# The first fifty microseconds of a fused attention and expert kernel: the order of its opening work

## The chip, the cores and the metric

The kernel runs on one core of a Trainium2 chip. The core has five engines that each run their own instruction list in order: the tensor engine (PE, matmuls and transposes), the vector engine (DVE), the scalar engine (ACT), GpSimd (POOL) and the sync engine (SP), which here only issues transfers. They wait for one another through semaphores. The metric is the device time of one execution in microseconds (us); lower is better. The kernel before takes 721.48 us (median of 3 runs, 721.1 to 725.26).

## The reference: what is computed

A block-sparse attention feeds a mixture of experts. Attention has 4 batches, 8 heads, 768 positions and a head width of 64; its mask keeps, for each block of 32 queries, the neighbouring key blocks, the first and the last block, and three sampled ones. Each of the 3072 resulting rows of 512 goes to the one expert of eight with the highest gate logit.

```python
scores = scale * np.matmul(q, k.transpose(0, 1, 3, 2))
mask = np.abs(blk_i - blk_j) <= window
mask = mask | (blk_i == 0) | (blk_j == 0) | (blk_i == n_blocks - 1) | (blk_j == n_blocks - 1)
for qb in range(n_blocks):
    for kb in sampled_blocks[qb]:
        mask[qb * block:(qb + 1) * block, kb * block:(kb + 1) * block] = True
scores = np.where(mask, scores, -1000000000.0)
attn = np.exp(scores - np.max(scores, axis=-1, keepdims=True))
attn = attn / (np.sum(attn, axis=-1, keepdims=True) + 1e-09)
x = np.matmul(attn, v)            # then (B, H, S, D) -> (B*S, H*D)
...
logits = x @ w_gate
expert_idx = np.argmax(logits, axis=1)
# per expert e, on its rows:  y = np.maximum(x @ w1[e], 0.0) @ w2[e]
return gate_w[:, None] * y
```

## The kernel before

Heads are worked on in 16 pairs, `pairs[n]`, and each pair in two halves of 384 queries: a step is (n, half). A step computes scores for six chunks of 128 keys (`scores`), takes their exponential, adds them up (`esum`), multiplies with v (`attend`), and a step later divides by the sums (`divide`). The mask is applied in one of two ways. Either a second pair of small matmuls adds a penalty to the scores (`oh` says which block a key belongs to, `pen` which blocks a query may not see), or, for the "late" chunks 0 to 2, POOL multiplies the exponential with a table of zeros and ones (`mask`), which `make_late` computes once. `ps_s` is a rotation of three buffers in PSUM, which the tensor engine writes.

```python
lend(lent, ps_s=3)
...
def load(b, pr):
    for src, nm in ((k, "k_sb"), (q, "q_sb")):
        t = ld.tile([P, NCH, 2, D], F32, name=nm)
        for hh in range(2):
            queue = nc.scalar if nm == "q_sb" and (b, pr) == (0, 0) else nc.sync
            queue.dma_start(t[:, :, hh, :], src[b, 2 * pr + hh].rearrange("(p c) d -> p c d", p=P))
    ...                                          # v on nc.sync

def make_mask(pool):
    ...                                          # samp_i fetched on nc.scalar
    load(0, 0)
    ...
    nc.vector.memset(oh[:], 1.0)
    for ... in (six bounds):
        nc.gpsimd.affine_select(out=allow[:], in_=allow[:], ...)
    nc.gpsimd.iota(kb_i[:], ...)
    for half in range(2):
        part = oh[half * D : (half + 1) * D]
        for base, cm, st, sp in ((0, -BLK, 1, NCH), (BLK - 1, BLK, -1, -NCH)):
            nc.gpsimd.affine_select(out=part, in_=part, ...)
    nc.vector.tensor_copy(kb[:], kb_i[:])
    nc.vector.tensor_copy(samp[:], samp_i[:, :, 0])
    for r in range(NR):
        nc.vector.scalar_tensor_tensor(allow[:], in0=kb[:], scalar=samp[:, r : r + 1], in1=allow[:], ...)
    nc.vector.tensor_copy(allow2[:, :NB], allow[:])
    nc.vector.tensor_copy(allow2[:, D : D + NB], allow[:])
    for c in range(30):                          # keeps the tensor engine at work
        nc.tensor.transpose(idle[:, 0, :P], ident[:], ident[:])
    for half in range(2):
        nc.tensor.matmul(bm[:, half, :CW], lhsT=allow2[:], rhs=oh[:NB, half * HC : (half + 1) * HC, :], ...)
    for half in range(2):
        nc.vector.tensor_scalar(pen[:, half * CW : (half + 1) * CW], bm[:, half, :CW], ...)

def make_mix():
    nc.scalar.dma_start(wg[:], moe_w_gate.rearrange("(c p) e -> p c e", p=P))
    nc.gpsimd.memset(mix[:], 0.0)
    for pr in range(NPR):
        nc.gpsimd.tensor_copy(mix[:, pr, :P], ident[:])
        nc.gpsimd.tensor_copy(mix[:, pr, P:], wg[:, pr, :])

def make_late():
    for j, c in enumerate(LATE):                 # LATE = (0, 1, 2)
        bm = upper["ps_s"].tile([P, 2, 512], F32, name="bm", tag="s")
        for half in range(2):
            nc.tensor.matmul(bm[:, half, :CW], lhsT=oh[:D, c, :], rhs=pen[:D, cols], ...)
        nc.vector.tensor_single_scalar(mask[:, j, :]..., bm[:, :, :CW], 0.0, op=ALU.is_ge)

def turn(b, pr, which):                          # 12 transposes of k or q into tp (a ps_s buffer), then
    for j in range(2):
        to, got = dst.rearrange("p (c j t) -> p j c t", j=2, t=D)[:, j], tp[:, j, :CW]...
        if (b, pr, which) == (0, 0, 1):
            nc.vector.tensor_copy(to, got)
        else:
            nc.scalar.copy(to, got)

def scores(n, half, c):
    late = c in LATE and 0 < n < NA              # NA = 12
    ...                                          # two matmuls per chunk, k with q (L252)
    for hh in range(0 if late else 2):           # the penalty (L255)
        nc.tensor.matmul(s[:, hh, :CW], lhsT=oh[r, c, :], rhs=pen[r, cols], ...)
    nc.scalar.activation(e, s[:, :, :CW], AF.Exp, scale=scale)            # L257
    if late:
        nc.gpsimd.tensor_tensor(e, e, m..., op=ALU.mult)                  # L261
    if c >= 3:
        ...                                      # sums on nc.vector (L267)

for which in range(2):
    turn(0, 0, which)
for i, (n, half) in enumerate(steps):
    ...                                          # loads two pairs ahead
    if 0 < i and n + 1 < len(pairs):
        turn(*pairs[n + 1], half)
    for c in range(NCH):
        scores(n, half, c)
    if i == 0:
        make_mix()
        route_consts()                           # small constants on POOL; `t` also uses nc.vector (L459, L460)
    if i > 0:
        divide(*steps[i - 1])                    # sums over keys by matmul (L290), reciprocal
    for c in ORDER:
        attend(n, half, c)
    if i == 0:
        make_late()
        turn(*pairs[1], 0)
    ...                                          # rows out, gates, then the experts
```

The lists of PE, DVE and POOL follow the order of the program text; that of ACT does so from the loop on.

Of the kernel before, what the change touches and what calls it, by code (L numbers as in the profile page):

```python
# [12 lines left out]
ALU = mybir.AluOpType  # L13
# [4 lines left out]
def kernel(  # L18
# [11 lines left out]
    nc = tc.nc  # L30
    P = 128
    B, H, S, D = q.shape
    BLK = 32
# [71 lines left out]
    def load(b, pr):  # L105
        got = []
        for src, nm in ((k, "k_sb"), (q, "q_sb")):
            t = ld.tile([P, NCH, 2, D], F32, name=nm)
            for hh in range(2):

                queue = nc.scalar if nm == "q_sb" and (b, pr) == (0, 0) else nc.sync
                queue.dma_start(t[:, :, hh, :], src[b, 2 * pr + hh].rearrange("(p c) d -> p c d", p=P))
            got.append(t)
        t = ld.tile([P, 2, NCH, D], F32, name="v_sb", bufs=3)
        nc.sync.dma_start(
            t.rearrange("p h c d -> p h (c d)"), v[b, 2 * pr : 2 * pr + 2].rearrange("h (p c) d -> p h (c d)", p=P),
        )
        got.append(t)
        loaded[(b, pr)] = got
# [17 lines left out]
    def make_mask(pool):  # L137

        halves = bass.DRamTensorHandle(sampled_blocks.tensor.name, (2 * NB * NR,), I32)
        samp_i = pool.tile([NB, NR, 2], I32, name="samp_i")  # L140
        nc.scalar.dma_start(
            samp_i.rearrange("a b c -> a (b c)"), bass.AP(tensor=halves, offset=0, ap=[[2 * NR, NB], [1, 2 * NR]]),
        )
        load(0, 0)

        warm = pool.tile([P, 1], F32, name="warm")
        nc.scalar.activation(warm[:], ones[:, :1], AF.Exp)

        allow = pool.tile([NB, NB], F32, name="allow")
        nc.vector.memset(allow[:], 1.0)  # L150
        nc.vector.memset(oh[:], 1.0)
        allow2 = pool.tile([NB, P], BF16, name="allow2")
        nc.vector.memset(allow2[:], 0.0)
        for base, cm, step, fill in (
            (1, -1, 1, 0.0), (1, 1, -1, 0.0), (-1, 1, 0, 1.0), (NB - 2, -1, 0, 1.0), (-1, 0, 1, 1.0), (NB - 2, 0, -1, 1.0),
        ):
            nc.gpsimd.affine_select(
                out=allow[:], in_=allow[:], compare_op=ALU.is_ge, fill=fill, base=base, channel_multiplier=cm,
                pattern=[[step, NB]],
            )  # L160
        kb_i = pool.tile([NB, NB], I32, name="kb_i")
        nc.gpsimd.iota(kb_i[:], pattern=[[1, NB]], base=0, channel_multiplier=0)
        for half in range(2):
            part = oh[half * D : (half + 1) * D]
            for base, cm, st, sp in ((0, -BLK, 1, NCH), (BLK - 1, BLK, -1, -NCH)):
                nc.gpsimd.affine_select(
                    out=part, in_=part, compare_op=ALU.is_ge, fill=0.0, base=base, channel_multiplier=cm,
                    pattern=[[st, NCH], [sp, P]],
                )
        kb = pool.tile([NB, NB], F32, name="kb")  # L170
        nc.vector.tensor_copy(kb[:], kb_i[:])
        samp = pool.tile([NB, NR], F32, name="samp")
        nc.vector.tensor_copy(samp[:], samp_i[:, :, 0])
        for r in range(NR):
            nc.vector.scalar_tensor_tensor(
                allow[:], in0=kb[:], scalar=samp[:, r : r + 1], in1=allow[:], op0=ALU.is_equal, op1=ALU.max,
            )
        nc.vector.tensor_copy(allow2[:, :NB], allow[:])
        nc.vector.tensor_copy(allow2[:, D : D + NB], allow[:])

        idle = upper["ps_s"].tile([P, 2, 512], F32, name="idle", tag="s")
        for c in range(30):
            nc.tensor.transpose(idle[:, 0, :P], ident[:], ident[:])
        bm = upper["ps_s"].tile([P, 2, 512], F32, name="bm", tag="s")
        for half in range(2):
            nc.tensor.matmul(
                bm[:, half, :CW], lhsT=allow2[:], rhs=oh[:NB, half * HC : (half + 1) * HC, :], start=True, stop=True,
            )
        for half in range(2):
            nc.vector.tensor_scalar(  # L190
                pen[:, half * CW : (half + 1) * CW], bm[:, half, :CW], scalar1=-MASKED, scalar2=MASKED, op0=ALU.mult, op1=ALU.add,
            )

    def make_mix():
        nc.scalar.dma_start(wg[:], moe_w_gate.rearrange("(c p) e -> p c e", p=P))
        nc.gpsimd.memset(mix[:], 0.0)
        for pr in range(NPR):
            nc.gpsimd.tensor_copy(mix[:, pr, :P], ident[:])
            nc.gpsimd.tensor_copy(mix[:, pr, P:], wg[:, pr, :])
# [21 lines left out]
    def turn(b, pr, which):  # L221

        src = loaded[(b, pr)][which]
        dst = work.tile([P, S], F32, name="qT" if which else "kT")
        turned.setdefault((b, pr), {})[which] = dst
        tp = upper["ps_s"].tile([P, 2, 512], F32, name="tp", tag="s")

        for c in range(NCH):
            for j in range(2):
                r = slice(j * D, (j + 1) * D)  # L230
                nc.tensor.transpose(tp[:, j, c * D : (c + 1) * D], src[r, c].rearrange("p h d -> p (h d)"), ident[r, r])  # L231
        for j in range(2):
            to, got = dst.rearrange("p (c j t) -> p j c t", j=2, t=D)[:, j], tp[:, j, :CW].rearrange("p (c t) -> p c t", t=D)

            if (b, pr, which) == (0, 0, 1):
                nc.vector.tensor_copy(to, got)  # L236
            else:
                nc.scalar.copy(to, got)

    rt = {}  # L240
    es, ops_, esums, xbs, s_alls = {}, {}, {}, {}, {}
# [1 line left out]
    def scores(n, half, c):  # L243

        b, pr = pairs[n]
        kT, qT = turned[(b, pr)][0], turned[(b, pr)][1]
        cols = slice(half * CW, (half + 1) * CW)
        late = c in LATE and 0 < n < NA
        s = upper["ps_s"].tile([P, 2, 512], F32, name="s")
        for hh in range(2):  # L250
            r = slice(hh * D, (hh + 1) * D)
            nc.tensor.matmul(s[:, hh, :CW], lhsT=kT[r, c * P : (c + 1) * P], rhs=qT[r, cols], start=True, stop=late)  # L252
        for hh in range(0 if late else 2):
            r = slice(hh * D, (hh + 1) * D)
            nc.tensor.matmul(s[:, hh, :CW], lhsT=oh[r, c, :], rhs=pen[r, cols], start=False, stop=True)  # L255
        e = e_slot(n, half, c)
        nc.scalar.activation(e, s[:, :, :CW], AF.Exp, scale=scale)  # L257
        es[(n, half, c)] = e
        if late:
            m = mask[:, LATE.index(c), cols]  # L260
            nc.gpsimd.tensor_tensor(e, e, m[:, None, :].to_broadcast([P, 2, CW]), op=ALU.mult)  # L261
        if c >= 3:
            if c == 3:
                esums[(n, half)] = work.tile([P, 2, CW], F32, name="esum")
            t = esums[(n, half)]
            for c_ in {3: (0,), 4: (4, 1), 5: (5, 2)}[c]:
                nc.vector.tensor_add(t[:], es[(n, half, 3)] if c == 3 else t[:], es[(n, half, c_)])  # L267
# [719 lines left out]
    for i, (n, half) in enumerate(steps):  # L987
        if half == 1 and n + 2 < len(pairs):
            load(*pairs[n + 2])
        if 0 < i and n + 1 < len(pairs):  # L990
            turn(*pairs[n + 1], half)
        for c in range(NCH):
            scores(n, half, c)
        if i == 0:
            make_mix()
            route_consts()
        if i > 0:
            divide(*steps[i - 1])
        for c in ORDER:
            attend(n, half, c)  # L1000
        if i == 0:
            make_late()
            turn(*pairs[1], 0)
        if "gates" in rt:
            gate_weights(*rt.pop("gates"))
        if n > 0:
            rows_out(n - 1, half)

        if (n, half) == (NA, 1):
            ranks("A", 0, TA)  # L1010
        if (n, half) == (NA + 1, 0):
            count("A")
            layout_a()
            for i_ in range(2):
                fetch(i_, 1)
                fetch(i_, 2)
        if (n, half) == (NA + 1, 1):
            slots_a()
        if n == NA + 2:
            one_hots("A", rt["slA"], TA, KA, half)  # L1020
        if (n, half) == (NA + 3, 0):
            tokens("A", TA, KA)
            for i_ in range(3):
                gather(i_)
        if n + 1 == len(pairs) and half == 1:
            turn_x(0)
# [171 lines left out]
```

## Time and profile before

| what | before |
|---|---|
| device time, median of 3 | 721.48 us (721.1 to 725.26) |
| profiled span | 720.0 us |
| PE busy | 695.5 us, 97% |
| DVE busy | 437.0 us, 61% |
| ACT busy | 271.7 us, 38% |
| POOL busy | 189.7 us, 26% |
| mean granted PE clock | 0.987 |

The profile is of one execution. A row of its order-of-time view gives the start, the time from the first to the last of so many like instructions, the engine, the line of the kernel, the operation, output and inputs, their shapes, the count, and in brackets how long the engine had been idle and what it had waited for. An engine name with q is its instruction queue, which issues transfers. A row of waits gives who waited for whom, the total, the number of times and the longest. A row of the stretches view gives the window, its length, the busy time of PE, its weight loads, DVE, ACT and POOL with instruction counts, the granted PE clock, and the share and rate of the DMA engines.

The chain of work that ended last, by engine:

```profile
PE 55%; issue 33%; POOL 5%; DVE 3%; DMA 1%; ACT 1%; POOLq 0%; ACTq 0%; another core or an unknown queue 0%; DVEq 0%
```

### The profile page before, as it was taken

The page shows a single profiled execution, that of the slowest core. Times are in us where ns is not written, and L with a number is a line of the kernel's source. Part 1 is how long each engine was busy: PE and PEld are TensorE (multiplying, and loading weights), DVE is VectorE, ACT ScalarE, POOL GpSimd, SP SyncE. Part 2 cuts the span into 40 slices and gives each one's busy share as a digit, 9 for nine tenths or more (in the row PEclk, how much of TensorE's full clock was granted, in tenths as well). Part 3 has the DMA queues.
Part 4 walks back from the last instruction along what each step waited for, and adds up shares of the span by engine and source line. Part 5 has one row for each costly group of instructions (what it writes and reads, how often), then busy time and mean ns, then how long its engine had stood idle before and what let it go on. Part 6 is the DMA issues. An engine that isn't in the chain of part 4 may idle for free.

```text
span 720.0 us, 12889 instructions
## 1 busy us (share of the span) xinstructions
PE 695.5 (97%) x5008; PEld 454.1 (63%) x5008; DVE 437.0 (61%) x828; ACT 271.7 (38%) x456; POOL 189.7 (26%) x180
## 2 busy tenths in 40 slices
PE   8699999999999999999999999999999999999993
PEld 5355555555555555555677776778687967777861
DVE  5399999999999998999748025820228012902200
ACT  3365675567566755765411110111111111111110
POOL 3344554565456540000202112101130013011210
PEclk9799999999999999999999999999999999999997
DMA  8122332233323322194378999996999499979950
GB/s 198 45 66 70 89 88 63 48 92 88 87 70 90 88 65 47 47 361 152 83 253 297 307 327 355 355 338 222 374 396 382 137 364 399 397 254 383 396 192 18
DMA packets 114569, 145.52 MB, mean 202 GB/s; under 512 B 56228, under 2 KB 72676, under 8 KB 114469
## 3 DMA queue, kind: packets, MB, share of 16 engines
q1 hardware_dynamic: 107968, 129.84, 54.6%
q0 software_dynamic: 4368, 14.02, 5.2%
q8 instruction: 53, 0.87, 0.5%
q10 hardware_dynamic: 2132, 0.41, 0.3%
q14 instruction: 48, 0.39, 0.2%
HBM read 131.47 MB, written 12.94 MB: 201 GB/s over the span
## 4 chain that ended last, share of the span: by engine, by line
PE 55%; issue 33%; POOL 5%; DVE 3%; DMA 1%; ACT 1%; POOLq 0%; ACTq 0%; another core or an unknown queue 0%; DVEq 0%
PE s L252 17%; PE op L277 17%; PE hp L833 6%; PE sp L290 4%; PE xr L310 3%; PE zp L847 3%; PE s L255 3%; PE tp L231 2%; POOL out_dram L862 2%; POOL xg L765 1%; DMA q_sb<-in_q_dram 1%; ACT ea L257 1%; DMA wg<-in_moe_w_gate_dram 1%; DVE orB L695 0%; POOL ea L885 0%
## 5 line engine op out<-in xcount | busy, mean ns | idle before, releaser
L261 POOL TENSOR_TENSOR ea<-ea,mask 128x768 f32<-128x768 f32 x66 | 120.4, 1851 | 116.9 <-ACT ea L257 101.5
L257 ACT ACTIVATE ea<-s 128x768 f32<-128x768 f32 x192 | 146.1, 815 | 9.4 <-PE s L255 6.1
L252 PE MATMUL s<-qT,kT 64*128 64x384 f32 x768 | 148.0, 492 | 1.3 <-DVE qT L236 1.2
L833 PEld LDWEIGHTS hp<-xgT,w 128*128 128x128 f32 x1216 | 138.5, 192 | 9.5 <-issue 6.4
L833 PE MATMUL hp<-xgT,w 128*128 128x128 f32 x1216 | 141.4, 276 | 2.6 <-ACT hT L840 1.6
L814 DVE STREAM_TRANSPOSE xgT<-xg 32x128 f32<-32x128 f32 x208 | 62.9, 302 | 128.5 <-DMA xg<-x_rows,gB 87.3
L267 DVE TENSOR_TENSOR esum<-esum,ea 128x768 f32<-128x768 f32 x128 | 125.4, 980 | 12.0
L277 PE MATMUL op<-ea,v_sb 128*64 128x384 f32 x768 | 129.3, 486 | 0.0
L847 PE MATMUL zp<-w,hT 128*128 128x512 f32 x256 | 112.7, 594 | 0.0
L277 PEld LDWEIGHTS op<-ea,v_sb 128*64 128x64 f32 x768 | 55.1, 137 | 68.8 <-issue 65.6
L252 PEld LDWEIGHTS s<-qT,kT 64*128 64x128 f32 x768 | 68.3, 189 | 41.6 <-ACT ea L257 17.0
L297 DVE RECIPROCAL r<-ss 128x128 f32<-128x128 f32 x96 | 82.2, 912 | 0.0
L847 PEld LDWEIGHTS zp<-w,hT 128*128 128x128 f32 x256 | 47.5, 190 | 54.6 <-issue 54.4
L840 ACT ACTIVATE hT<-hp 128x512 f32<-128x512 f32 x36 | 21.5, 598 | 116.9 <-PE hp L833 96.7
L862 POOL DMA_INDIRECT out_dram<-zo,sB x14 | 14.1, 1006 | 166.0 <-ACT zo L852 119.0
L282 ACT COPY oT<-op 128x384 f32<-128x384 f32 x32 | 15.4, 480 | 104.2 <-PE op L277 104.2
L852 ACT ACTIVATE zo<-zp,xg 128x512 f32<-128x512 f32 x16 | 11.0, 689 | 100.7 <-PE zp L847 100.7
L267 DVE TENSOR_TENSOR esum<-ea 128x768 f32<-128x768 f32 x32 | 35.7, 1117 | 14.8 <-ACT ea L257 14.7
L255 PE MATMUL s<-pen,oh 64*128 64x384 bf16 x252 | 41.6, 326 | 0.0
L940 DVE STREAM_TRANSPOSE ea<-ea 32x128 f32<-32x128 f32 x84 | 21.7, 285 | 28.8 <-DMA ea<-x_rows,gB 28.1
L298 DVE TENSOR_TENSOR oT<-oT,r 128x384 f32<-128x384 f32 x32 | 30.2, 943 | 1.1
L310 PEld LDWEIGHTS xr<-mix,oT 128*64 128x64 f32 (+1 forms) x372 | 24.0, 139 | 10.7 <-issue 10.6
(282 smaller groups left out, 546.3 us busy)
## 6 DMA issues: line engine op xcount, KB each, us to landing
w<-in_moe_w_dram SPq DMA_DIRECT2D x50, 2048.0 KB
k_sb<-in_k_dram SPq DMA_DIRECT2D x32, 192.0 KB
v_sb<-in_v_dram SPq DMA_DIRECT2D x16, 384.0 KB
x_rows<-xb SPq DMA_DIRECT2D x16, 384.0 KB
q_sb<-in_q_dram SPq DMA_DIRECT2D x30, 192.0 KB
sums<-ss SPq DMA_DIRECT2D x32, 3.0 KB
q_sb<-in_q_dram ACTq DMA_DIRECT2D x2, 192.0 KB
xg<-x_rows,gB POOLq DMA_INDIRECT x15
```

Source lines behind the costliest of these rows:

```text
L252: nc.tensor.matmul(s[:, hh, :CW], lhsT=kT[r, c * P : (c + 1) * P], rhs=qT[r, cols], start=True, stop=late)
L255: nc.tensor.matmul(s[:, hh, :CW], lhsT=oh[r, c, :], rhs=pen[r, cols], start=False, stop=True)
L257: nc.scalar.activation(e, s[:, :, :CW], AF.Exp, scale=scale)
L261: nc.gpsimd.tensor_tensor(e, e, m[:, None, :].to_broadcast([P, 2, CW]), op=ALU.mult)
L267: nc.vector.tensor_add(t[:], es[(n, half, 3)] if c == 3 else t[:], es[(n, half, c_)])
L277: nc.tensor.matmul(op[hh * D : (hh + 1) * D, :], lhsT=v_sb[:, hh, c, :], rhs=e[:, hh, :], start=(c == ORDER[0]), stop=(c == ORDER[-1]),)
L297: nc.vector.reciprocal(r[:, m * P : (m + 1) * P], ss[:, m * P : (m + 1) * P])
L298: nc.vector.tensor_mul(oT[:], oT[:], r[:])
L310: nc.tensor.matmul(xr[j * M_ : (j + 1) * M_, m, :], lhsT=oT[:, m * P + j * M_ : m * P + (j + 1) * M_], rhs=mix[:, pr, :], start=True, stop ...
L814: nc.vector.transpose(xT[d, :, t], xg[t, :DM].rearrange("p (c q) -> p c q", c=DB)[:, :, d])
L833: nc.tensor.matmul(hp[:, m, :], lhsT=st[i]["w1"][:, c, fb * P : (fb + 1) * P], rhs=st[i]["xT"][:, c, :], start=(c == 0), stop=(c == DB - 1),)
L847: nc.tensor.matmul(zp[:], lhsT=st[i]["hT"][:, fb, :], rhs=st[i]["w2"][:, fb, :], start=(fb == 0), stop=(fb == FB - 1),)
```

## The change

It rearranges the opening; what is computed stays the same.

- The tables of the late masks are made after the third chunk of the very first scores, not after the first attention. With them at hand, the second step (0, 1) also uses the late form: no penalty matmuls for its chunks 0 to 2, but three multiplications on POOL.
- The gate weights `wg` are fetched on the sync queue right after the first pair's loads, so that POOL need not wait for them in `make_mix`.
- The table `oh` is made for 64 partitions and copied to the other 64 by ACT, which leaves POOL two selects fewer.
- The first q loads move from the scalar queue to the sync queue, behind k and ahead of v.
- The first pair's transposes are copied out by halves of the columns rather than by interleaved parts, so that the first scores need one copy of k and one of q.
- The warming transposes are 22, not 30.

```diff
@@ load
-                queue = nc.scalar if nm == "q_sb" and (b, pr) == (0, 0) else nc.sync
-                queue.dma_start(t[:, :, hh, :], src[b, 2 * pr + hh].rearrange("(p c) d -> p c d", p=P))
+                nc.sync.dma_start(t[:, :, hh, :], src[b, 2 * pr + hh].rearrange("(p c) d -> p c d", p=P))
@@ make_mask
         load(0, 0)
+        nc.sync.dma_start(wg[:], moe_w_gate.rearrange("(c p) e -> p c e", p=P))
...
-        nc.vector.memset(oh[:], 1.0)
+        nc.vector.memset(oh[:D], 1.0)
...
-        for half in range(2):
-            part = oh[half * D : (half + 1) * D]
-            for base, cm, st, sp in ((0, -BLK, 1, NCH), (BLK - 1, BLK, -1, -NCH)):
-                nc.gpsimd.affine_select(
-                    out=part, in_=part, compare_op=ALU.is_ge, fill=0.0, base=base, channel_multiplier=cm,
-                    pattern=[[st, NCH], [sp, P]],
-                )
+        for base, cm, st, sp in ((0, -BLK, 1, NCH), (BLK - 1, BLK, -1, -NCH)):
+            nc.gpsimd.affine_select(
+                out=oh[:D], in_=oh[:D], compare_op=ALU.is_ge, fill=0.0, base=base, channel_multiplier=cm,
+                pattern=[[st, NCH], [sp, P]],
+            )
+        nc.scalar.copy(oh[D:], oh[:D])
...
-        for c in range(30):
+        for c in range(22):
@@ make_mix
-        nc.scalar.dma_start(wg[:], moe_w_gate.rearrange("(c p) e -> p c e", p=P))
@@ turn
+        to, got = dst.rearrange("p (c j t) -> p j c t", j=2, t=D), tp[:, :, :CW].rearrange("p j (c t) -> p j c t", t=D)
         for j in range(2):
-            to, got = dst.rearrange("p (c j t) -> p j c t", j=2, t=D)[:, j], tp[:, j, :CW].rearrange("p (c t) -> p c t", t=D)
-            if (b, pr, which) == (0, 0, 1):
-                nc.vector.tensor_copy(to, got)
+            if (b, pr) == (0, 0):
+                cs = slice(j * HC, (j + 1) * HC)
+                (nc.vector.tensor_copy if which else nc.scalar.copy)(to[:, :, cs], got[:, :, cs])
             else:
-                nc.scalar.copy(to, got)
+                nc.scalar.copy(to[:, j], got[:, j])
@@ scores
-        late = c in LATE and 0 < n < NA
+        late = c in LATE and (n, half) != (0, 0) and n < NA
@@ the loop
         for c in range(NCH):
             scores(n, half, c)
+            if (i, c) == (0, 2):
+                make_late()
...
         if i == 0:
-            make_late()
             turn(*pairs[1], 0)
```

## The prediction

> **What bounds the kernel now.** I first read the page's slices of the span and its list of what the tensor engine (PE) waited for over the whole run.
>
> ```profile
> PE   8699999999999999999999999999999999999993
> ...
> PEclk9799999999999999999999999999999999999997
> ```
>
> ```profile
> PE tp L231 <- DVE mask L207: 6.0, 1, 6.0
> PE hp L833 <- ACT hT L840: 1.6, 4, 0.5
> PE idle L183 <- POOL ident L73: 1.4, 1, 1.4
> PE s L252 <- DVE qT L236: 1.2, 1, 1.2
> ```
>
> PE is busy in every slice except the first two and the last, and the granted clock falls in the second slice. The largest wait of the run by far is one 6.0 us wait on the masks of line 207. From 45 us to 500 us PE is never idle for a noticeable time, so time saved ahead of that passes through to the end, and nothing else in this change can. So I read the order-of-time view of the first 50 us.
>
> ```profile
> 15.44 0.42 ACTq L195 DMA_DIRECT2D wg<-in_moe_w_gate_dram  x1
> ...
> 19.13 0.66 POOL L199 COPY mix<-wg 128x8 f32<-128x8 f32 x1 [11.57 <-DMA wg<-in_moe_w_gate_dram]
> ...
> 19.35 1.15 PE L206 MATMUL bm<-pen,oh 64*128 64x384 bf16 x6
> ...
> 25.28 0.18 DVE L459 TENSOR_SCALAR t<-t 128x24 int32<-128x24 int32 x1 [5.55 <-POOL t L456]
> ...
> 25.45 2.68 DVE L207 TENSOR_SCALAR mask<-bm 128x768 bf16<-128x768 f32 x3
> ...
> 26.46 0.91 PE L231 MATMUL tp<-ident,k_sb 64*128 64x64 f32 x12 [5.96 <-DVE mask L207]
> ```
>
> Read from the bottom. PE cannot transpose the second pair's k at 20.5 because all three `ps_s` buffers hold `bm`. Those are freed by the vector engine's (DVE) mask operations, which stand in its program behind `t` (L459). `t` needs the GpSimd (POOL) iota of L456, the last but few of 6 us of POOL constants, and these stand behind the copies of `wg`, whose transfer was issued only at 15.44 and awaited at 19.13. The late transfer, carried through two in-order engines, becomes PE's gap. The stretches view shows the after-effect:
>
> ```profile
> 20.50:26.50 6.00, 0.04 (x2) 0.04 (x2) 1.22 (x4) 0.00 (x0) 4.93 (x33) 0.63 0.00 1
> 26.50:35.30 8.80, 8.71 (x60) 4.97 (x60) 2.24 (x3) 5.61 (x9) 0.29 (x3) 0.67 0.39 89
> ```
>
> The column after POOL is the clock. One-us windows show 0.50 from 22 us until about 32.2 us: PE works at half rate for 5.7 us after it has resumed (26.46 to 32.2), which loses about 2.9 us more.
>
> Lastly the opening, where PE waits for `allow` and then for q:
>
> ```profile
> 2.95 3.65 POOL L166 TENSOR_SCALAR_AFFINE_SELECT oh<-oh 64x768 bf16<-64x768 bf16 x4
> ...
> 3.94 2.68 DVE L175 SCALAR_TENSOR_TENSOR allow<-kb,samp,allow 24x24 f32<-24x24 f32 x3
> ...
> 7.31 0.49 PE L186 MATMUL bm<-oh,allow 24*128 24x384 bf16 x2 [0.67 <-DVE allow L179]
> ...
> 8.49 0.59 PE L231 MATMUL tp<-ident,q_sb 64*128 64x64 f32 x12 [0.17 <-DMA q_sb<-in_q_dram]
> ...
> 9.11 1.02 DVE L236 COPY qT<-tp 128x384 f32<-128x384 f32 x2 [0.25 <-PE tp L231]
> ...
> 10.28 0.92 PE L252 MATMUL s<-qT,kT 64*128 64x384 f32 x4 [1.21 <-DVE qT L236]
> ```
>
> A DVE operation on 24x24 elements takes 0.89 us here: each ends with the POOL select beside it (POOL starts at 2.95, 3.88, 4.80, 5.73; DVE at 3.94, 4.80, 5.73). By the chain of waits q landed at 8.35.
>
> **What the Trainium skill says.** "SBUF — State Buffer", section "Who interferes with whom": DVE and GpSimd share one port pair as an exclusive lock, taken by a DVE copy or scalar operation in a two-port mode or by one with two SBUF inputs against a GpSimd operation that reads. The 0.89 us per tiny operation agrees. "VectorE: DVE Perf Modes", section "Why PSUM operands drop a tier": a PSUM source rules the two-port mode out. The mask operations agree: three of 0.949 to 0.951 us, while POOL worked beside the first and not the last. So moving them beside POOL's constants should not slow them. "DMA: Bandwidth & Descriptors", section "Queues, rings and completion order": each DMA engine goes round robin between the queues that have work. The trace agrees: in 3.5 to 4.0 us the scalar queue moved 506 packets and the sync queue 26, and in 6.5 to 7.0 it was 82 to 197, with v already in the sync queue. "TensorE: Matmul & The Clock Gate", section "What's actually happening": an idle window drops PE to half clock and sustained work restores it; the 0.50 from 22 us to 32.2 us agrees.
>
> **The change part by part.**
>
> (a) *Half the table's selects.* Two selects (2 x 0.91 us) leave POOL, which ends `oh` at 4.74. The following 0.55 us memset and 0.29 us copy of `mix` move up. DVE's second and third step on `allow` then lock against those instead: ends about 5.4 and 5.7, the two casts about 6.0. `bm` starts about 6.05 instead of 7.31. The new scalar-engine (ACT) copy of 64x768 runs about 4.8 to 5.6, when ACT is idle (4.01 us before 8.36). The 22 warming transposes end near 5.5 (the thirty end at 6.64; the last six took 0.82 us, so eight fewer take off 1.1 us): not in the way.
>
> (b) *q on the sync queue ahead of v.* 3072 packets of 256 B must land for k and q. With both queues the trace counts some 2540 of these by 5.5 us; the rest at some 900 per us ends near 6.1. The last q packets ran until about 7.75 and q was released at 8.35, so 0.6 us of tail: landed near 6.7 if q no longer shares with v. Then k transposes start at 6.5, q's at 7.15, and end at 7.75.
>
> (c) *Column halves.* The first scores need only the first of the two 0.5 us qT copies: 7.8 + 0.5 + 0.15 = 8.5 instead of 10.28. Gain of (a) to (c): 1.8 us, my least certain term (0.8 to 2.2).
>
> (d) *Masks amid the scores.* The exponentials are 0.81 us each and begin 1.1 us after the first score: 9.6, 10.4, 11.2, 12.0. The three `bm` pairs (0.32 each) follow the third score at 10.95 and wait for exponential ends: last one at about 12.4. Mask operations (0.95) at 11.5, 12.4, 13.4; scores 3, 4, 5 each need one of their buffers: 12.5, 13.4, 14.4 to 15.2. Scores to attention took 5.04 us before (10.28 to 15.32) and takes about 6.8 now: 8.5 + 6.8 = 15.3. So the move costs 1.75 us here, 1.15 of it paid at 19.35 before. Attention 4.03 us: 19.35, the same moment as before.
>
> (e) *No wait.* The second pair is transposed at once, at full clock: 2 x 0.52 us (the chain's figure at 40.04) to 20.5. Before: 19.35 + 1.15 + 5.96, then 1.86 to 28.32.
>
> (f) *Masked second block.* Scores of (0,1) are now 3 x 0.65 + 3 x 0.81 = 4.4 us, having shed 6 x 0.16 us; the buffers wait for ACT (kT and qT copies 0.86 each, then the exponentials), about 0.2 us more: the sums' matmul (L290) starts at about 25.1 instead of 35.30.
>
> POOL takes 3 x 1.87 us for this. With `wg` queued behind v it should land near 8 to 9; copies and constants (1.7 + 4.4 us up to the iota) end near 15; `t` follows DVE's last sum near 19.5; the last 1.2 us of constants end before 21. The first masked block's exponential ends near 22.5, POOL multiplies until 28.2, and attention wants the third at 29.2. It fits with 1 us to spare.
>
> Sum: 35.30 - 25.1 = 10.2 us. From there everything is as before, including the weight fetches, which PE's progress releases. 721.48 - 10.2 = 711.3; I allow 0.2 for frayed edges: **711.5 us**, 1.4% less.
>
> **The rivals.** *The head start does not come*: q lands near 8.3 regardless, since DMA engines are busy from 2.7 us on either way. For it: the stretch at 155 GB/s near 4.5 us, which I cannot explain. Against: v's packets ran before q was done. It leaves 0.5 us of 1.8: 712.8. *GpSimd becomes the bound*: `wg` in 32-byte runs took 3.6 us from issue alone; behind loads it might land at 13 us or later, pushing the constants past 22.5 and the multiplies into attention. POOL has 7 us of slack there, so it would take more than that: 712 to 714. *The masks stall the scores or the warm clock is lost* (eight fewer warming transposes): about 3.4 us of half rate would cost 1.7: 713.2. *DVE takes over*: it was 95% busy from 100 to 200 us, and PE's gap had let it catch up. By my times its sums of (0,1) end near 29.8, when PE leaves attention, as before (39.7 against 39.97): no loss expected, but 1 to 2 us if they pile up.
>
> **Range and chances.** The 5.96 us wait and 2.9 us of half clock are firm; the shed 1.0 us nearly so. Uncertain are the head start (-1.0, +0.4), stalls (1), POOL (1) and the runs' own spread (721.1 to 725.26). I take 709.3 to 714.8. A gain over 2% needs below 707.05, or 4 us beyond my sum: 3%. Slower by 2%: 1%. Within 2%: 96%.
>
> **What would show it.** In the changed profile: no PE wait on line 207's mask beyond 0.5 us, a clock of 1.00 from 20 to 35 us; the first scores at 8.5 and the L290 sums at 25.1; mask operations at 11 to 14; q landed below 7; POOL's first multiply by 23. Wrong would be a new PE wait on POOL near 27 us, or a gain at 25 us that is gone at 260.

## The result, and the profile after

The changed kernel takes 712.02 us (median of 4 runs, 711.38 to 712.32) against 722.34 us for the kernel before in the same comparison: a ratio of 0.985 with a 95% interval of 0.9818 to 0.9883. The prediction was 711.5, in a range of 709.3 to 714.8. The profiled span fell from 720.0 to 710.6 us.

The slices of the span of the changed kernel, tensor engine (PE) and granted clock:

```profile
PE   8999999999999999999999999999998999999993
...
PEclk9999999999999999999999999999999999999997
```

The dip in the second slice is gone from both rows. What PE waited for over the whole run, longest first:

```profile
PE hpu L949 <- DMA w<-in_moe_w_dram: 3.5, 2, 1.9
PE idle L181 <- POOL ident L73: 1.4, 1, 1.4
PE hp L831 <- ACT hT L838: 1.4, 3, 0.5
PE s L250 <- DVE qT L234: 0.7, 1, 0.7
```

The 6.0 us wait on the masks has vanished. In first place stands a wait for expert weights that the profile of before did not show; more of it below. In order of time, the lines that answer to the chain shown of before:

```profile
4.42 0.47 SPq L143 DMA_DIRECT2D wg<-in_moe_w_gate_dram  x1
...
8.97 0.19 POOL L196 COPY mix<-wg 128x8 f32<-128x8 f32 x1 [3.40 <-DMA wg<-in_moe_w_gate_dram]
...
11.84 2.69 DVE L204 TENSOR_SCALAR mask<-bm 128x768 bf16<-128x768 f32 x3 [2.70 <-PE bm L203]
...
19.61 0.59 PE L228 MATMUL tp<-ident,k_sb 64*128 64x64 f32 x12
...
22.67 5.57 POOL L259 TENSOR_TENSOR ea<-ea,mask 128x768 f32<-128x768 f32 x3 [1.31 <-ACT ea L255]
...
25.26 0.87 PE L288 MATMUL sp<-esum,ones 128*64 128x384 f32 x4
```

The weights are there at 8.97 instead of 19.13, the mask operations run at 11.84, PE transposes the second pair at 19.61 without a wait, and the sums' matmul, the mark that the prediction counted by, starts at 25.26 (25.1 predicted) instead of 35.30. The opening:

```profile
3.93 1.35 DVE L173 SCALAR_TENSOR_TENSOR allow<-kb,samp,allow 24x24 f32<-24x24 f32 x3
...
6.23 0.49 PE L184 MATMUL bm<-oh,allow 24*128 24x384 bf16 x2
...
7.49 0.59 PE L228 MATMUL tp<-ident,q_sb 64*128 64x64 f32 x12 [0.24 <-DMA q_sb<-in_q_dram]
...
8.82 0.92 PE L250 MATMUL s<-qT,kT 64*128 64x384 f32 x4 [0.74 <-DVE qT L234]
```

The first scores start at 8.82 instead of 10.28. In the stretches view of the changed kernel, from the mark backwards (PE busy, then its weight loads, DVE, ACT, POOL, and the clock):

```profile
8.80:15.59 6.79, 6.49 (x43) 3.25 (x43) 3.80 (x5) 3.99 (x5) 5.00 (x31) 1.00 1.06 256
15.59:19.61 4.02, 4.02 (x27) 1.63 (x25) 3.73 (x5) 0.86 (x2) 0.00 (x0) 1.00 0.41 71
19.61:25.26 5.65, 5.65 (x56) 2.97 (x55) 0.91 (x4) 5.50 (x10) 3.69 (x9) 1.00 0.65 139
```

The clock is full in each. From the start of the second pair's transposes to the mark it is 5.65 us (8.84 before), in which PE shows no idle time. At the last sums' matmul, in the profiles at 343.6 against 353.6 us, the gain is still 10.0 us; at the end it is 9.4.

### The profile page after: what moved, and what is told of

Read it like the earlier page. It is cut to its first block, busy times and chain, and to the rows that moved or that the text cites. A ratio compares the mean times of both kernels' runs of the same rounds, so it can differ in the third digit from the quotient of the medians.

```text
span 710.6 us, 12866 instructions
## 1 busy us (share of the span) xinstructions
PE 691.6 (97%) x4994; PEld 451.1 (63%) x4994; DVE 434.3 (61%) x828; ACT 271.6 (38%) x457; POOL 193.5 (27%) x181
## 4 chain that ended last, share of the span: by engine, by line
PE 56%; issue 34%; POOL 4%; DVE 3%; DMA 1%; ACT 0%; SPq 0%; POOLq 0%; another core or an unknown queue 0%; DVEq 0%
PE s L250 18%; PE op L275 17%; PE hp L831 6%; PE sp L288 4%; PE xr L308 3%; PE zp L845 3%; PE s L253 3%; PE tp L228 2%; POOL out_dram L860 2%; POOL xg L763 1%; DMA q_sb<-in_q_dram 1%; DVE orB L693 0%; POOL ea L883 0%; POOL ea L928 0%; ACT ea L255 0%
## 5 line engine op out<-in xcount | busy, mean ns | idle before, releaser
L259 POOL TENSOR_TENSOR ea<-ea,mask 128x768 f32<-128x768 f32 x69 | 126.9, 1866 | 106.0 <-ACT ea L255 106.0
L250 PE MATMUL s<-qT,kT 64*128 64x384 f32 x768 | 146.3, 489 | 0.7 <-DVE qT L234 0.7
L265 DVE TENSOR_TENSOR esum<-esum,ea 128x768 f32<-128x768 f32 x128 | 129.0, 1008 | 13.3 <-DVE esum L265 1.0
L296 DVE TENSOR_TENSOR oT<-oT,r 128x384 f32<-128x384 f32 x32 | 28.5, 890 | 1.1
```

The costliest lines, as they stand in the source:

```text
L296: nc.vector.tensor_mul(oT[:], oT[:], r[:])
```

## The experiments

Each is read at three places: the first scores, the mark (the first sums' matmul) and the time. The place of the first scores moves by up to 0.8 us between runs with the landing of q and the end of the warming transposes, so the distance between first scores and mark is the sharper figure: 25.02 us before (35.30 - 10.28), 16.44 after (25.26 - 8.82). These places come from one profiled run of each kernel. A ratio given with a time may differ by about 0.001 from the quotient of the two medians.

### One part alone: the gate weights fetched early

```diff
  load(0, 0)
+ nc.sync.dma_start(wg[:], moe_w_gate.rearrange("(c p) e -> p c e", p=P))
@@ make_mix
- nc.scalar.dma_start(wg[:], moe_w_gate.rearrange("(c p) e -> p c e", p=P))
```

> The kernel before with one part of the change alone: the gate weights fetched on the sync queue behind the first pair's loads. Mark: start of the first step's sums matmul (35.30 us before, 25.26 after the whole change). Theory (PE's gap is the late transfer carried through GpSimd and the vector engine): the constants are done by 15 us, the mask operations start when bm is there and the last sum is done, near 20.1, PE transposes again near 21.1 at full clock; mark near 28.2, time 7 us below before, 715 us. Rival (the gain is the move of the masks and the masked second block, the transfer only helps): mark at 33 or later, time within 2.5 us of before.

PE's list in order of time, of this kernel:

```profile
19.85 1.15 PE L206 MATMUL bm<-pen,oh 64*128 64x384 bf16 x6
21.40 0.59 PE L231 MATMUL tp<-ident,k_sb 64*128 64x64 f32 x12 [0.40 <-DVE mask L207]
22.26 0.59 PE L231 MATMUL tp<-ident,q_sb 64*128 64x64 f32 x12 [0.28 <-DVE mask L207]
...
27.99 0.87 PE L290 MATMUL sp<-esum,ones 128*64 128x384 f32 x4
```

The 5.96 us wait shrinks to 0.40 and 0.28, the mark stands at 27.99, the time is 716.59 (714.64 to 718.73, the profiled run 714.68; ratio to before 0.9921, 0.9896 to 0.9945). From first scores (10.78 here) to mark it is 17.21 us: one moved transfer gives 7.8 of the 8.6 us that the whole change takes off this distance. The rival, for which the moved masks carry the gain and the transfer only helps, is out.

### The change without that part: the gate weights late again

```diff
- nc.sync.dma_start(wg[:], ...)          # after load(0, 0)
@@ make_mix
+ nc.scalar.dma_start(wg[:], ...)
```

> The kernel after, with the gate weights fetched late on the scalar queue again (inside make_mix), all else as after. Theory (either cut alone opens PE's gap, but the masked second block then needs GpSimd early): sums matmul still near 25.3, no PE wait on the masks; GpSimd's constants end near 27.9, its three multiplies near 33.5, and the second attention waits for them, so that the third pair's transposes start near 34.4 instead of 29.93: 4.4 us lost, 716.5 us. Rival (moving the masks alone is enough, the transfer is hidden): third pair's transposes near 30, 712 us.

PE's list, of this kernel:

```profile
24.54 0.87 PE L288 MATMUL sp<-esum,ones 128*64 128x384 f32 x4
25.24 0.81 PE L275 MATMUL op<-ea,v_sb 128*64 128x384 f32 x4
28.23 5.14 PE L275 MATMUL op<-ea,v_sb 128*64 128x384 f32 x20 [2.18 <-POOL ea L259]
33.30 0.59 PE L228 MATMUL tp<-ident,k_sb 64*128 64x64 f32 x12
```

GpSimd (POOL) of this kernel:

```profile
24.83 0.16 POOL L454 IOTA t<- 128x24 int32 x1
...
26.54 5.54 POOL L259 TENSOR_TENSOR ea<-ea,mask 128x768 f32<-128x768 f32 x3
```

From first scores (8.10) to mark it is 16.44 us, exactly as in the changed kernel: with the masks ahead of `t` in the vector engine's program, the late weights no longer reach PE at that place. But POOL starts to multiply at 26.54, attention stands still for 2.18 us and then waits on between its matmuls, and the third pair's transposes come 25.20 us after the first scores instead of 21.11. The time is 716.96 (0.9923, 0.9894 to 0.9952; the profiled run 715.39). So either cut alone removes PE's big gap, and their gains do not add up. By the wait on POOL, it is the masked second block that makes the early weights necessary again; the kernel with late weights and an unmasked second block, which would show it, was not run.

### PE kept at work in the gap of the kernel before

```diff
  make_late()
+ fill = ps_x.tile([P, CW], F32, name="fill", tag="xr")
+ for _ in range(36):
+     nc.tensor.transpose(fill[:, :P], ident[:], ident[:])
  turn(*pairs[1], 0)
```

> The kernel before with 36 extra transposes of the identity into an unused PSUM tile behind the mask matmuls, so that PE is at work in its gap and otherwise waits as before. Theory (the half clock after the gap costs by itself): transposes resume at 26.5 as before but at full clock, sums matmul at 32.7 instead of 35.30, time 2.6 us below before, 719.7. Rival (the copies and exponentials on the scalar engine set the pace there, the clock costs nothing): sums matmul at 35 or later, time within 0.5 us of before.

PE of this kernel:

```profile
22.19 1.15 PE L206 MATMUL bm<-pen,oh 64*128 64x384 bf16 x6
23.27 4.15 PE L1005 MATMUL fill<-ident 128*128 128x128 f32 x36
28.70 0.59 PE L231 MATMUL tp<-ident,k_sb 64*128 64x64 f32 x12 [1.28 <-DVE mask L207]
29.56 0.59 PE L231 MATMUL tp<-ident,q_sb 64*128 64x64 f32 x12 [0.28 <-DVE mask L207]
30.43 0.92 PE L252 MATMUL s<-qT,kT 64*128 64x384 f32 x4 [0.27 <-DVE mask L207]
...
35.47 0.87 PE L290 MATMUL sp<-esum,ones 128*64 128x384 f32 x4
```

The mark itself tells nothing here, since this run's opening was late and partly at half clock (q came later, and the clock stood at 0.50 from 12 to 14 us):

```profile
12.00:13.00 1.00, 1.00 (x6) 0.46 (x4) 0.00 (x0) 0.00 (x0) 0.00 (x0) 0.50 0.94 290
13.00:14.00 1.00, 1.00 (x7) 0.71 (x6) 0.00 (x0) 0.61 (x1) 0.00 (x0) 0.50 1.02 334
```

From the second pair's transposes to the mark it is 6.77 us, against 8.84 in the kernel before: the half clock cost 2.07 us. Two waits of 0.28 and 0.27 us for masks appear, which slow PE had covered. The time is 721.09 against 723.23 (0.997, 0.9959 to 0.9982), 2.1 us. The theory's 2.6 was a little too much (it is the 2.07 and the two waits together), the rival's zero is out.

### The second step with the penalty again

```diff
- late = c in LATE and (n, half) != (0, 0) and n < NA
+ late = c in LATE and 0 < n < NA
```

> The kernel after, with the second step's chunks 0 to 2 masked by the penalty matmuls again and no GpSimd multiplies there. By my sum in the prediction the six matmuls shed are worth 1.0 us less 0.2 of waits: 0.8 us slower, sums matmul at 26.1. Theory after seeing the profile (PE waits for buffers in that step anyway, 0.47 us): 25.7, 0.45 us slower, 712.5. Rival (GpSimd's early multiplies hold attention up, so the penalty form is as good or better): third pair's transposes at 29.9 or earlier, time equal or less than after.

First scores at 8.29, mark at 24.87: 16.58 us, 0.14 more than after. Third pair's transposes 21.25 us after the first scores (21.11 after). The time is 712.17 (0.9857, 0.9828 to 0.9886), as after. So six penalty matmuls less are worth 0.14 us: the changed step has 4.85 us from scores to mark (25.26 - 20.41), this one 4.99 (24.87 - 19.88). The expectation's 1.0 us was itself too large, since it counted 0.16 us for each matmul. The two matmuls of a chunk run together, and the pair takes 0.16 us; in the changed kernel, the penalty form of the first step shows it:

```profile
9.54 0.36 PE L253 MATMUL s<-pen,oh 64*128 64x384 bf16 x2
9.70 0.84 PE L250 MATMUL s<-qT,kT 64*128 64x384 f32 x4
```

Three pairs are 0.48 us. The rest went into waits for buffers and copies of ACT: between the transposes and the mark, the weight loads of the scores wait 1.9 us for ACT in the changed kernel and 0.5 us here.

The masked form has a price on the vector engine (DVE). Its sums of this step, first of the changed kernel, then of this one:

```profile
24.80 1.93 DVE L265 TENSOR_TENSOR esum<-ea 128x768 f32<-128x768 f32 x1 [4.74 <-ACT ea L255]
26.83 5.40 DVE L265 TENSOR_TENSOR esum<-esum,ea 128x768 f32<-128x768 f32 x4
```

```profile
24.27 0.96 DVE L265 TENSOR_TENSOR esum<-ea 128x768 f32<-128x768 f32 x1 [4.75 <-ACT ea L255]
25.33 4.00 DVE L265 TENSOR_TENSOR esum<-esum,ea 128x768 f32<-128x768 f32 x4
```

Beside POOL's multiplies the five sums end 7.43 us after the first begins, without them 5.06 us. PE did not wait for it: the next sums' matmul starts at 34.86, and the sums end at 32.23.

### The first q loads on the scalar queue again

```diff
- nc.sync.dma_start(t[:, :, hh, :], ...)
+ queue = nc.scalar if nm == "q_sb" and (b, pr) == (0, 0) else nc.sync
+ queue.dma_start(t[:, :, hh, :], ...)
```

> The kernel after, with the first q loads on the scalar queue again, so that q shares the DMA engines with v. Theory (q on one queue ahead of v is what brings it 1.0 us sooner: released 7.35 after, 8.35 before): q released near 8.3, first scores near 9.8 instead of 8.82, sums matmul near 26.2, 713 us. Rival (q's landing is set by the bytes alone): released near 7.4, no change.

PE of this kernel:

```profile
5.73 0.49 PE L185 MATMUL bm<-oh,allow 24*128 24x384 bf16 x2 [0.31 <-DVE allow L178]
7.31 0.59 PE L229 MATMUL tp<-ident,k_sb 64*128 64x64 f32 x12 [1.09 <-DMA k_sb<-in_k_dram]
8.41 0.59 PE L229 MATMUL tp<-ident,q_sb 64*128 64x64 f32 x12 [0.51 <-DMA q_sb<-in_q_dram]
```

The chain that ended last has q's transfer (start, length) in the changed kernel as

```profile
2.95 4.40 DMA q_sb<-in_q_dram
```

and here as

```profile
2.16 6.11 DMA q_sb<-in_q_dram
```

q is released at 8.27 (7.35 after), and k too is late. Packets of both queues now run side by side: from 5.0 to 7.0 us the scalar queue moved 658 packets, the sync queue 818. First scores 9.74, mark 26.17, as the theory said. The time, 714.92 (0.9893, 0.9873 to 0.9912), is 2 us more than that explains. In the profiled run most of it lies in the experts: after a 2.08 us wait for weights the clock fell for a while (0.94 on average from 610 to 640 us) and a group of matmuls took 6.26 instead of 4.5 us. Whether the other runs lost it in the same place is open.

### The first copies interleaved again

```diff
- (nc.vector.tensor_copy if which else nc.scalar.copy)(to[:, :, cs], got[:, :, cs])
+ (nc.vector.tensor_copy if which else nc.scalar.copy)(to[:, j], got[:, j])
```

> The kernel after, with the first pair's k and q copied out by interleaved parts again, so that the first scores need both copies. Theory: first scores 0.5 us later (9.3), but the mask operations queue behind the same copies, so sums matmul at 25.7, 0.45 us slower. Rival (the exponentials and the mask operations set the pace of that step, so half a microsecond at its start is absorbed): sums matmul within 0.15 us of 25.26.

PE waits 1.24 us for qT instead of 0.74, so a half copy saves 0.5 us at that wait. In this run q came sooner (its transposes began at 7.18), so the first scores stand at 8.96 and the mark at 25.40, 16.44 us apart: nothing was absorbed on the way. The time is 713.12 (0.9871, 0.985 to 0.9891); its interval overlaps that of the change, so the 0.5 us is a reading of the profile, not of the times.

### All four selects of the block table, with 22 and with 30 warming transposes

```diff
- nc.vector.memset(oh[:D], 1.0)
+ nc.vector.memset(oh[:], 1.0)
- for base, cm, st, sp in (...):
-     nc.gpsimd.affine_select(out=oh[:D], in_=oh[:D], ...)
- nc.scalar.copy(oh[D:], oh[:D])
+ for half in range(2):
+     part = oh[half * D : (half + 1) * D]
+     for base, cm, st, sp in (...):
+         nc.gpsimd.affine_select(out=part, in_=part, ...)
@@ the second of the two kernels also
- for c in range(22):
+ for c in range(30):
```

> The kernel after, with all four selects of the block table on GpSimd again and no copy by the scalar engine. Theory (the vector engine's steps on allow end with the GpSimd instruction beside them): the three steps take 2.7 us again instead of 1.35, allow's second cast ends near 7.2 instead of 5.68, its matmul starts at 7.3, first scores near 9.8, sums matmul near 26.2, 713 us. Rival (q's landing at 7.35 sets the start, the table is off the path): first scores within 0.3 us of 8.82.

> The kernel after, with all four selects on GpSimd and 30 warming transposes. With 22 transposes the same kernel had PE idle for 1.75 us ahead of the table and half clock until 14.6 us. Theory (two separate costs: the table is 1.1 us later, and the short warming lets the clock fall): first scores near 9.9 again, but at full clock, sums matmul at 26.3 instead of 28.72, time near 713. Rival (the clock fell by chance or for another reason): sums matmul near 28.7, time near 715.4.

The stretches of the kernel with 22:

```profile
5.00:7.20 2.20, 0.53 (x5) 0.29 (x3) 2.13 (x4) 0.00 (x0) 2.06 (x3) 1.00 0.96 250
7.20:14.60 7.40, 6.57 (x44) 3.91 (x45) 2.07 (x6) 2.48 (x4) 5.29 (x32) 0.55 1.16 266
```

And with 30:

```profile
5.00:7.20 2.20, 2.20 (x15) 2.11 (x13) 2.13 (x4) 0.00 (x0) 2.06 (x3) 1.00 1.14 256
7.20:14.60 7.40, 6.34 (x60) 3.64 (x60) 4.11 (x9) 3.29 (x5) 5.29 (x32) 1.00 1.19 270
```

In both the table's matmul starts at 7.28 or 7.29, as in the kernel before: two selects are worth about 1 us of table. With 22 transposes PE then stood idle for 1.75 us, and the clock was 0.55 on average from 7.2 to 14.6 us; the mark came at 28.72 and the time is 715.43 (0.9898, 0.9881 to 0.9916). With 30 the clock held, the mark came at 25.89, the time is 712.52 (0.9853, 0.9826 to 0.988). So the shorter warming without the earlier table costs 2.8 us at the mark; with it, the clock stayed at 1.00 there in every profile.

### Thirty warming transposes in the changed kernel

```diff
- for c in range(22):
+ for c in range(30):
```

> The kernel after, with 30 warming transposes instead of 22. Theory: 22 of them took 4.85 us at half rate and ended at 6.30, past allow at 5.68, so they already were in the way of the table's matmul; eight more end near 7.4 to 8.1, first scores 0.8 to 1.5 us later, sums matmul at 26.0 to 26.7. Rival (the clock comes up as in the kernel before, where 30 end at 6.64, and q's landing is later): first scores within 0.3 us of 8.82.

The table's matmul at 7.76, first scores at 9.93, mark at 26.36, 16.43 us apart: eight more transposes delay the opening by 1.1 us in this profile. The time is 712.59 (0.9856, 0.9838 to 0.9875), 0.6 us above the change, which the intervals do not separate.

### The masks spread over the first scores

The changed kernel makes three masks in a row behind the third chunk. There PE waits for the exponentials to free buffers, and then for the masks. One of the three fits into PE's wait for qT (`make_late` here takes the numbers of the masks that it is to make):

```diff
  for c in range(NCH):
+     if (i, c) == (0, 0):
+         make_late((0,))
      scores(n, half, c)
      if (i, c) == (0, 2):
-         make_late()
+         make_late((1,))
+     if (i, c) == (0, 3):
+         make_late((2,))
```

> The kernel after, with the three masks not made together after the third chunk of the first scores but spread: the first ahead of the first scores (while PE waits for the copy of qT), the second after the third chunk, the third after the fourth. Theory (after the change the first step is set by PE's bm matmuls and by the mask operations that its last three scores wait for): one bm pair (0.32 us) falls into PE's 0.74 us wait at 8.1, and the mask operations are no longer three in a row; first scores to attention in 5.9 instead of 6.77 us, sums matmul 0.9 us earlier against the first scores (16.4 to 15.6), time 0.8 us below after. Rival (the exponentials on the scalar engine set the step, the order of the masks is indifferent): the distance from first scores to sums matmul stays within 0.2 us of 16.44, time as after.

> The kernel after once more, beside the others on the same chip: 712.0 us, sums matmul within 0.7 us of 25.26 (q's landing moves the opening from run to run), 16.44 us from first scores to sums matmul.

This kernel's stretch from the end of the q transposes to attention:

```profile
8.20:14.73 6.53, 6.33 (x42) 3.22 (x42) 3.92 (x7) 4.39 (x7) 5.51 (x29) 1.00 1.14 268
```

The changed kernel, run beside it:

```profile
8.20:15.66 7.46, 6.49 (x43) 3.26 (x43) 4.47 (x7) 4.46 (x7) 5.02 (x31) 1.00 1.13 262
```

PE is idle for 0.20 us of this stretch instead of 0.97. Both have their first scores at 8.88 and 8.89; attention follows 5.85 instead of 6.77 us later, and the mark stands at 24.40 instead of 25.33. The time is 710.7 us (710.39 to 711.85, 5 runs; ratio to before 0.9825, 0.9803 to 0.9848) against 711.89 for the changed kernel (0.9846, 0.9819 to 0.9873). The two intervals overlap, so the 0.93 us is shown by the profiles and only suggested by the times; the lower median fits. It has the lowest median of all versions measured here.

## Why the prediction was right

*The chain.* PE's gap was indeed the late transfer, handed on by two in-order engines. Moving the transfer alone (first experiment) leaves 0.68 us of the 5.96 us wait; putting it back (second) brings the stall back in another place, at POOL's multiplies.

*(a) to (c), the opening.* 1.46 us came of 1.8 predicted, and by the terms' own experiments the parts are of the predicted kind: late table, q on its old queue and old copies cost 1.0, 0.9 and 0.5 us each at the point they touch. They do not add up, since the opening waits for whichever is last. Three sub-steps were off. The 22 warming transposes did not end near 5.5 but at 6.30 in the profiled run, because they took 0.22 us each (4.85 us), twice the 0.11 us of those in the filled gap; the recorded clock does not show it, it reads 1.00 there. So the table's matmul started at 6.23 rather than 6.05. In three other profiles the 22 did end at 5.4 to 5.5. The lock of DVE against POOL's memset did not come: the last cast ended at 5.68, not at 6.0. That the table's start was nearly met is therefore luck. And q was not landed near 6.7 but released at 7.35; in other runs of kernels with the same loads it was there by 6.8 or 7.2. The packet counts that the prediction gave for turns between two queues, 506 to 26 and 82 to 197, show both at work but no equal turns.

*(d) masks amid the scores.* First scores to attention: 6.77 us, predicted 6.8; mask operations 11.84 to 14.53, predicted 11.5 to 14.3, 2.69 us for the three with POOL busy alongside (2.68 before), as the prediction took from the "Trainium skill", "VectorE: DVE Perf Modes", section "Why PSUM operands drop a tier": a PSUM source rules out the mode that needs both SBUF read ports. The sum counted the waits that three in a row bring, without asking whether they could be had for less; the spread version shows that 0.9 us of them could.

*(e) no wait.* The transposes start at 19.61, predicted 19.35; there is no wait on a mask. The two groups take 0.80 us (19.61 to 20.41), predicted 1.15.

*(f) masked second block.* The distance from transposes to mark is 5.65 us, predicted 5.75 (19.35 to 25.1). That it came so close is luck: the transposes were 0.35 us shorter than predicted, and the scores 0.25 us longer (4.85 against 4.6). "Shed 6 x 0.16 us" and "the shed 1.0 us" were wrong: a pair takes 0.16 us, so it is 0.48, as the prediction's own 3 x 0.65 + 3 x 0.81 has it. The waits took 0.47 us (4.85 less these 4.38), not 0.2; with the penalty they took 0.13 (4.99 less 6 x 0.81), so that 0.14 us of gain is left. The sum at the mark went by the 4.4 us and not by the 1.0.

*The half clock.* "Loses about 2.9 us more" was a mis-sized term: 2.07 us by the filled gap, since slow PE hid some 0.55 us of waits on masks. It did not enter the sum, which went by the mark.

*POOL.* Weights at 8.97 (8 to 9 predicted), constants done by 21.4 (21), multiplies 22.67 to 28.24 (22.5 to 28.2). The rival of GpSimd as the bound was false for the change and true for it with late weights.

*DVE.* Its sums of (0,1) end at 32.2, not near 29.8, because they ran beside POOL's multiplies (1.93 us for the first instead of 0.96). PE did not wait, so the rival of DVE taking over was false, but with 2.4 us less to spare than the prediction thought.

*The warm clock.* It held in the change. Where it was lost, with 22 transposes and the late table, it cost 2.8 us at the mark, more than the 1.7 of that rival.

*From the mark on.* "From there everything is as before" held to within 0.6 us: from the last sums' matmul to the end the profile has 366.4 us before and 367.0 after. Only the profile of before shows no wait for expert weights; the other twelve have 1.5 to 3.8 us of it, and lie between 366.5 and 368.9 us in this stretch. The filled-gap kernel, which starts its experts as late as before, has 3.3 us and 367.0, so an earlier start is not the cause, and the changed kernel run again has 3.1 us and 366.6, so the wait is mostly made up elsewhere. What sets it is open.

*The base.* By the medians of one comparison the gain is 10.3 us (722.34 to 712.02), by the two profiles 9.4. 721.48 us was at the low end for the kernel before: 25 later runs gave 720.83 to 726.26 with a median of 723.23. The changed kernel stayed within 710.91 to 714.31 in nine. The profile of before is of a run of 721.85 us, nearly as low, so that base and sum belong together: of the 0.5 us between 711.5 and 712.02, 0.16 came at the mark and 0.6 after it, less the 0.2 allowed for. The filled gap and the four-select kernel show that the opening can run at half clock and what that costs; that this is what spreads the runs of before is likely, but not shown.

## What to carry to other kernels

When one engine waits long, follow the releaser's own program upwards: here a matrix unit waited for masks, the masks stood behind an unrelated constant, the constant behind a copy, and the copy behind a small transfer that a fourth engine came to issue only at 15.44 us, 8 us after the copy could have run. Issuing that transfer with the first loads gave, by itself, most of the gain. When several cuts go through the same chain, measure each alone: they do not add up, and one may be what makes the other necessary. Here the masked second block leaned on the early weights, and was itself worth 0.14 us at the mark and nothing in the times.

## What was unexpected of the hardware

- *Little warming and a pause of 1.75 us lost the clock.* In the four-select kernel PE had worked from 1.45 to 5.53 us, paused until 7.28, and ran at 0.55 on average from 7.2 to 14.6 us; 30 transposes instead of 22, which also close the pause, avoided it. The shorter work alone does not do it: in the kernel with q on the scalar queue PE had worked for nearly as long (3.98 us), and pauses of 0.31, 1.09, 0.51 and 0.74 us with work between them left the clock at 1.00. Nor do 30 transposes protect from it: in the filled-gap kernel, after 5.06 us of them, pauses of 0.78, 1.17 and 1.21 us were followed by 0.50 from about 11.6 us. And in the kernel before, PE stopped at 20.50 us and the clock was down from about 22 us. What exactly decides, these runs do not tell.
- *A second queue made a transfer land later.* q issued 0.77 us earlier on the scalar queue (1.49 against 2.26 us) was released 0.92 us later (8.27 against 7.35), its packets running among those of k and v. None of the four profiles with q on the scalar queue has it before 8.27. The "Trainium skill", "DMA: Bandwidth & Descriptors", section "Issuing engines are not separate DMA queues", says that a second issuing engine only saves the issue time; here it cost more than it saved.
- *Removing PE work bought next to nothing in a step whose buffers another engine frees*: of 0.48 us of matmuls, 0.14 us.
- *Two small matmuls took the time of one*: the two penalty matmuls of a chunk, each on its own half of the rows, together take 0.16 us (9.54 to 9.70); the two that make a mask's table, both on the same half, take 0.30 us (11.38 to 11.68 in the kernel with spread masks).
